# Linear attention ahead of two feed-forward layers: regrouping four kinds of small fp32 matmuls

## Chip, cores and metric

One core of a Trainium2 chip runs the whole program. The metric is the device time of one execution in microseconds (us).

## What is computed

The reference chains three layers; the change is in the first.

```python
def _attn_ref(q, k, v, w_phi):            # q, k, v: 4 batches x 8 heads x 576 x 64; w_phi 64 x 128
    def phi(x):
        proj = np.einsum('bhsd,df->bhsf', x, w_phi)
        proj = proj - np.max(np.abs(proj), axis=-1, keepdims=True)
        return np.concatenate([np.exp(proj), np.exp(-proj)], axis=-1)
    q_p, k_p = (phi(q), phi(k))
    kv = np.einsum('bhsf,bhsd->bhfd', k_p, v)
    z = np.sum(k_p, axis=2)
    num = np.einsum('bhsf,bhfd->bhsd', q_p, kv)
    den = np.einsum('bhsf,bhf->bhs', q_p, z)[..., None] + 1e-06
    return num / den
```

Its output, 2304 tokens of 512 features, goes through a feed-forward layer (512 to 2048 and back, the hidden values squared after the relu) and then through eight gated feed-forward experts (512 to 1024 and back) whose gates are balanced in eight rounds.

## The kernel before

Attention works in 16 units of two heads each (four units make a batch). A unit has ten steps: `kT` and `kp` (turn k, project it, take exponentials: tiles `ek`, made in three pieces, the last of 64 rows), `qst`, `qT` and `qp` (split, turn and project q, take the maximum over features with GpSimd's all-reduce, take exponentials: four tiles `eq`), `kv` (function `kv_sum`), `kz` (`kv_turn`), `num` (`numerators`), `rec` and `fin`. A list written by hand, `OFFS`, with a period `TU` of 17.54, sets in which order the steps are traced. A scheduler then fixes the order on each engine at build time: it takes what is ready, in the order of tracing. On the chip every engine runs its list in order.

`kv_sum` adds up `v^T ek` for two heads in the upper and lower 64 partitions of a PSUM tile `kvp`, over five row tiles (four of 128 rows and one of 64), and the column sums of `ek` in `zp`, whose stationary operand is 32 columns of ones: four of these matmuls fill the 128 partitions. Each fp32 matmul of this kind is two instructions in the trace. Before, the row tiles go in pairs, `kvp` first and then `zp` for the pair. ScalarE copies both to `kvs`; `kv_turn` transposes them into `kzp`, from which VectorE makes `kv` and `z`.

`numerators` makes for each half `c` of the tokens the numerators `psn` (64 columns of `kv`, two heads side by side) and the denominators `psd` (32 columns of `z`, four matmuls side by side). ScalarE copies them to `nm` and `dn`. Two DMAs gather the denominators in `comp`, VectorE inverts them, one DMA writes them to DRAM (`rden`), two read them back spread over partitions (`rb`), and `finish` multiplies, rounds to `xh` (ScalarE) and keeps the rest in `xl` (VectorE).

PSUM tiles `kvp`, `zp`, `kzp`, `psn` and `psd` share three banks (`pc`, `PCB = 3`). The four `eq` tiles of a unit have four buffers (`EQB = 4`), so those of the next unit take the place of the ones that `psn` and `psd` have read.

The matmuls of the first feed-forward pass (`first_l1`, `first_l2`, PSUM tile `ps`, by blocks of 288 tokens) come after attention in the order of tracing and fill gaps in it. `HOLD` keeps some blocks back until `kv` of a named unit is through; its anchor is the last `zp` matmul that `kv_sum` returns. The weights' decoding (lines 198 to 204) sits on VectorE beside attention.

Of the kernel before, what the change touches and what calls it, by code (L numbers as in the profile page):

```python
# [8 lines left out]
F32 = mybir.dt.float32  # L9
# [11 lines left out]
def tile_features_attention__moe__sinkhorn_moe(  # L21
# [18 lines left out]
    nc = tc.nc  # L40
    P = 128
    B, H, S, D = q.shape
    NT, DM = out.shape
    NF = w_phi.shape[1]
# [10 lines left out]
    MT = S // P  # L55
# [39 lines left out]
    pc = a1.enter_context(tc.tile_pool(name="pc", bufs=PCB, space=PSUM, reuse_waits="tile"))  # L95
# [13 lines left out]
    ones = const.tile([P, P], F32, name="ones")  # L109
# [27 lines left out]
    def load_v(u):  # L137
        load_kv(u, v, "v", VAB)
# [195 lines left out]
    def kv_sum(u, eks):  # L334


        t = nat.pop(("v", u))
        kvp = pc.tile([P, 512], F32, tag="pc", name="kvp")
        zp = pc.tile([P, 512], F32, tag="pc", name="zp")

        def rows(i, h):
            r = P if i < MT else R0
            return r, eks[i // GT][:r, i % GT, h].rearrange("p a f -> p (a f)")

        for g in range(0, MT + 1, 2):
            tiles = range(g, min(g + 2, MT + 1))
            for i in tiles:
                for h in range(2):
                    r, e = rows(i, h)
                    nc.tensor.matmul(  # L350
                        kvp[h * D : (h + 1) * D, : 2 * NF], t[:r, i, h], e, start=(i == 0), stop=(i == MT)
                    )
            for i in tiles:
                for h in range(2):
                    r, e = rows(i, h)
                    q0 = 32 * (2 * (i % 2) + h)
                    ins = nc.tensor.matmul(  # L357
                        zp[q0 : q0 + 32, : 2 * NF], ones[:r, :32], e, start=(i < 2), stop=(i >= MT - 1)
                    )
        load_v(u + VAB)  # L360
        kvs = ab.tile([P, 2, 2, NF], F32, tag="kvs", name="kvs")
        nc.scalar.copy(kvs[:, 0].rearrange("p a f -> p (a f)"), kvp[:, : 2 * NF])
        nc.scalar.copy(kvs[:, 1].rearrange("p a f -> p (a f)"), zp[:, : 2 * NF])
        return kvs, ins.ins

    def kv_turn(u, kvs):
# [30 lines left out]
    def numerators(u, kz, eqs):  # L397

        kv, z = kz
        nm = ab.tile([P, 2, HALF], F32, tag="nm", bufs=NMB, name="nm")  # L400
        dn = ab.tile([P, 2, HALF], F32, tag="dn", name="dn")
        for c in range(2):
            ps = pc.tile([P, 512], F32, tag="pc", name="psn")
            for a in range(2):
                for h in range(2):
                    nc.tensor.matmul(  # L406
                        ps[h * D : (h + 1) * D, :HALF], kv[:, a, h * D : (h + 1) * D], eqs[2 * c + h][:, a],
                        start=(a == 0), stop=(a == 1),
                    )
            nc.scalar.copy(nm[:, c], ps[:, :HALF])  # L410
            ps = pc.tile([P, 512], F32, tag="pc", name="psd")
            for a in range(2):
                for h in range(2):
                    q0 = 32 * (2 * h + a)
                    nc.tensor.matmul(  # L415
                        ps[q0 : q0 + 32, :HALF], z[:, a, h], eqs[2 * c + h][:, a], start=True, stop=True
                    )
            nc.scalar.copy(dn[:, c], ps[:, :HALF])
        comp = ab.tile([P, 2, NT2], F32, tag="comp", bufs=1, name="comp")
        for a in range(2):  # L420
            nc.sync.dma_start(comp[:, a], dn[32 * a : P : 64].rearrange("p c s -> p (c s)"))
        return nm, comp
# [18 lines left out]
    def first_l1(pool, t0, n, fs=range(NFT)):  # L441
        return [split_square(pool, layer1(0, f, t0, n), n, HALF) for f in fs]
# [33 lines left out]
    def s_kv(u):  # L476
        U[u]["kvs"], U[u]["kvi"] = kv_sum(u, U[u].pop("ek"))
# [4 lines left out]
    def s_num(u):  # L482
        U[u]["nm"], U[u]["comp"] = numerators(u, U[u].pop("kz"), U[u].pop("eq"))
# [18 lines left out]
    for u in range(NU):  # L502
        t = u * TU
# [9 lines left out]
    for i, (t0, n) in enumerate(halves[:-2]):  # L513
        with ExitStack() as es:
            if i in HOLD:
                es.enter_context(tc.issue_after(U[HOLD[i][0]][HOLD[i][1]]))
            g = ahead + first_l1(hp, t0, n, range(len(ahead), NFT))
# [12 lines left out]
    with tc.tile_pool(name="hp1t", bufs=1, reuse_waits="tile") as hpt:  # L530
        g = [ahead + first_l1(hp, *halves[-2], range(len(ahead), NFT)), first_l1(hpt, *halves[-1])]
# [195 lines left out]
    for p in range(1, N1):  # L727
# [10 lines left out]
        for bi, (t0, n) in enumerate(blocks):  # L738
            g = []
# [294 lines left out]
    for n in range(NN):  # L1034
        l2 = layer2(n)
        if n + 1 < NN:
            l1 = layer1(n + 1)
            p, q = order[n + 1]
# [75 lines left out]
```

## Time and profile before

| | |
|---|---|
| median of 3 runs | 2109.71 us (2109.64 to 2115.81) |
| the profiled execution | 2112.68 us, of which the span is 2110.9 us |
| mean granted TensorE clock over the span | 0.991 |
| PE busy, share of the span | 98% |
| attention: first projection to last `xl` | 6.9 us to 306.5 us |

The page gives for each engine its busy time. PE are the matmuls, PEld the weight loads, DVE is VectorE, ACT ScalarE and POOL GpSimd. In a timeline each line has the start, the time to the end of the last instruction of the group, the engine, the line of the kernel, the operation, out<-in, the weights' shape (rows*columns), the moving operand, and how many instructions there are. A time in square brackets is how long the engine stood idle before it, and what ended the wait. Matmuls overlap, so the distance from start to start says what one costs.

### The profile page before, as it was taken

The numbers are of one execution on the slowest core, as the hardware profiler recorded it, in microseconds if no ns is written. First come the engines' busy times: TensorE is split into PE (matmuls) and PEld (weight loads), VectorE is DVE, ScalarE is ACT, GpSimd is POOL, SyncE is SP. The second block draws the span as 40 slices with busy tenths as digits, with TensorE's granted clock in tenths as the row PEclk, the third lists the DMA queues.
The fourth block names the chain that finished last, engine by engine and source line by source line (L and its number), as shares of the span: only waits on it lengthen the run. The fifth ranks groups of instructions, "written<-read, shape, count | busy, mean of one in ns | idle before, by whom it ended". The sixth has DMA issues, their size and how long they took to land.

```text
span 2110.9 us, 31778 instructions
## 1 busy us (share of the span) xinstructions
PE 2070.3 (98%) x12411; PEld 1933.7 (92%) x12411; DVE 1737.5 (82%) x2162; ACT 873.6 (41%) x1503; POOL 773.3 (37%) x425
## 2 busy tenths in 40 slices
PE   8999999999999899999999999999999999999998
PEld 5556679888999899999999999999999999999998
DVE  5888665776556787999989889899898998989986
ACT  6786744222233554433434334343343333433332
POOL 3343300010104444444544435444444444444431
PEclk9999999999999999999999999999999999999999
DMA  4444241100134557667766677666766667666663
GB/s 116 103 108 120 72 126 60 60 31 31 55 143 173 200 178 243 195 243 247 229 220 212 227 250 224 228 217 219 252 225 220 225 223 242 224 227 225 221 200 122
DMA packets 184052, 376.40 MB, mean 178 GB/s; under 512 B 73440, under 2 KB 114272, under 8 KB 183904
## 3 DMA queue, kind: packets, MB, share of 16 engines
q1 hardware_dynamic: 183904, 374.38, 53.9%
q8 instruction: 99, 1.62, 0.3%
q14 instruction: 49, 0.40, 0.1%
HBM read 349.26 MB, written 24.93 MB: 177 GB/s over the span
## 4 chain that ended last, share of the span: by engine, by line
PE 87%; DVE 7%; DMA 3%; ACT 1%; issue 1%; SPq 1%; POOL 0%; DVEq 0%; ACTq 0%
PE psa L855 31%; PE psb L855 31%; PE ps L241 6%; PE ps L242 6%; PE ps L243 6%; PE kvp L350 1%; DMA rb<-rden 1%; PE psn L406 1%; PE zp L357 1%; DVE xl L591 1%; PE psg L632 1%; DMA rden<-comp 1%; PE psd L415 1%; DVE xh L591 1%; DVE acc L971 1%
## 5 line engine op out<-in xcount | busy, mean ns | idle before, releaser
L855 PE MATMUL psa<-xl,xh 128*128 128x384 f32 x2400 | 446.8, 335 | 6.4 <-DVE xl L591 2.5
L855 PE MATMUL psb<-xl,xh 128*128 128x384 f32 x2400 | 444.2, 334 | 2.9 <-DVE xl L591 2.1
L855 PEld LDWEIGHTS psa<-xl,xh 128*128 128x128 f32 x2400 | 419.5, 188 | 8.1 <-DVE xl L591 2.9
L855 PEld LDWEIGHTS psb<-xl,xh 128*128 128x128 f32 x2400 | 418.3, 188 | 3.5 <-DVE xl L591 2.4
L883 POOL TENSOR_TENSOR t<-r,r 128x768 f32<-128x768 f32 x96 | 208.3, 2170 | 500.0 <-DVE r L923 453.1
L883 POOL TENSOR_TENSOR t<-r,t 128x768 f32<-128x768 f32 x96 | 236.6, 2464 | 5.6 <-DVE r L923 1.9
L591 DVE TENSOR_TENSOR xl<-t,xl 128x768 fp32r<-128x768 f32 x128 | 185.1, 1446 | 1.7 <-ACT xl L590 1.7
L971 DVE TENSOR_TENSOR acc<-psb,acc 128x768 f32<-128x768 f32 x163 | 155.0, 951 | 38.2 <-PE psb L855 34.7
L971 DVE TENSOR_TENSOR acc<-psa,acc 128x768 f32<-128x768 f32 x161 | 153.0, 950 | 38.6 <-PE psa L855 35.5
L855 PE MATMUL psb<-xl,w2v 128*128 128x384 f32 x960 | 180.3, 335 | 0.0
L855 PE MATMUL psa<-xl,w2v 128*128 128x384 f32 x960 | 179.7, 334 | 0.0
L590 ACT CAST xl<-t 128x768 fp32r<-128x768 f32 x128 | 107.4, 839 | 152.8 <-POOL t L883 62.3
L855 PEld LDWEIGHTS psb<-xl,w2v 128*128 128x128 f32 x960 | 168.0, 188 | 0.0
L855 PEld LDWEIGHTS psa<-xl,w2v 128*128 128x128 f32 x960 | 167.5, 188 | 0.0
L590 ACT CAST xl<-r 128x768 fp32r<-128x768 f32 x96 | 80.6, 839 | 156.1 <-PE psa L855 79.2
L390 POOL PARTITION_ALL_REDUCE eq<-eq x64 | 91.0, 1465 | 136.9 <-ACT eq L389 136.9
L591 DVE TENSOR_TENSOR xl<-r,xl 128x768 fp32r<-128x768 f32 x96 | 136.6, 1423 | 2.8 <-ACT xl L590 2.8
L241 PE MATMUL ps<-xh,w0h 128*128 128x288 f32 (+3 forms) x384 | 133.5, 348 | 3.2 <-ACT r L262 2.9
L242 PE MATMUL ps<-xl,w0h 128*128 128x288 f32 (+3 forms) x384 | 131.5, 343 | 0.0
L243 PE MATMUL ps<-xh,w0l 128*128 128x288 f32 (+3 forms) x384 | 131.5, 344 | 0.0
L661 POOL TENSOR_TENSOR s<-wf 128x512 f32<-128x512 f32 x32 | 44.5, 1391 | 227.3 <-PE ps L243 82.4
L242 PE MATMUL ps<-gl,w1h 128*128 128x288 f32 (+3 forms) x384 | 126.3, 336 | 0.0
(193 smaller groups left out, 3832.2 us busy)
## 6 DMA issues: line engine op xcount, KB each, us to landing
xl<-xv SPq DMA_DIRECT2D x329, 768.0 KB
wf<-in_moe_w_dram SPq DMA_DIRECT2D x32, 1024.0 KB
gate<-prT SPq DMA_DIRECT2D x45, 384.0 KB
xv<-xvs SPq DMA_DIRECT2D x14, 768.0 KB
raw<-in_moe_w_in_dram SPq DMA_DIRECT2D x16, 512.0 KB
raw<-in_moe_w_out_dram SPq DMA_DIRECT2D x16, 512.0 KB
xv<-xl SPq DMA_DIRECT2D x7, 768.0 KB
qnat<-in_q_dram SPq DMA_DIRECT2D x16, 288.0 KB
```

The lines of the kernel that those rows point to most:

```text
L241: nc.tensor.matmul(ps, ah, bh, start=first, stop=False)
L242: nc.tensor.matmul(ps, ah, bl, start=False, stop=False)
L243: nc.tensor.matmul(ps, al, bh, start=False, stop=last)
L350: nc.tensor.matmul(kvp[h * D : (h + 1) * D, : 2 * NF], t[:r, i, h], e, start=(i == 0), stop=(i == MT))
L357: ins = nc.tensor.matmul(zp[q0 : q0 + 32, : 2 * NF], ones[:r, :32], e, start=(i < 2), stop=(i >= MT - 1))
L390: nc.gpsimd.partition_all_reduce(eq[:, 1], eq[:, 0], P, bass_isa.ReduceOp.absmax)
L590: nc.scalar.copy(v[:, 0], src)
L591: nc.vector.tensor_sub(v[:, 1], src, v[:, 0].bitcast(F32))
L661: nc.gpsimd.tensor_tensor(s1, a(2, 1), a(2, 2), ALU.add)
L855: ins = nc.tensor.matmul(ps[:, x, :NB], w[:, wi, k, cs], b[:, bi, k], start=first and k + i == 0, stop=k == KH - 1 and i == 2, skip_group_ ...
L883: nc.gpsimd.tensor_tensor(t[nm], x, y, ALU.subtract)
L971: latest["dve"] = nc.vector.tensor_add(o, ps, o).ins
```

## The change

`kv_sum` now puts both sums in the two halves of one bank, `kvz`; it does all matmuls of `kvp` and then all of `zp`, from the last row tile (64 rows) to the first, and `zp` is tied behind the last `kvp`. One ScalarE copy of 128x512 takes the place of two of 128x256. `numerators` does both halves' `psn`, then both halves' `psd`, with the second half and the second head first.

```diff
-        kvp = pc.tile([P, 512], F32, tag="pc", name="kvp")
-        zp = pc.tile([P, 512], F32, tag="pc", name="zp")
+        kvz = pc.tile([P, 2, 2 * NF], F32, tag="pc", name="kvz")
+        kvp, zp = kvz[:, 0], kvz[:, 1]
...
-        for g in range(0, MT + 1, 2):
-            tiles = range(g, min(g + 2, MT + 1))
-            for i in tiles:
-                for h in range(2):
-                    r, e = rows(i, h)
-                    nc.tensor.matmul(
-                        kvp[h * D : (h + 1) * D, : 2 * NF], t[:r, i, h], e, start=(i == 0), stop=(i == MT)
-                    )
-            for i in tiles:
+        for i in range(MT, -1, -1):
+            for h in range(2):
+                r, e = rows(i, h)
+                ins = nc.tensor.matmul(
+                    kvp[h * D : (h + 1) * D], t[:r, i, h], e, start=(i == MT), stop=(i == 0)
+                )
+        with tc.issue_after(ins.ins):
+            for i in range(MT, -1, -1):
                 for h in range(2):
                     r, e = rows(i, h)
                     q0 = 32 * (2 * (i % 2) + h)
                     ins = nc.tensor.matmul(
-                        zp[q0 : q0 + 32, : 2 * NF], ones[:r, :32], e, start=(i < 2), stop=(i >= MT - 1)
+                        zp[q0 : q0 + 32], ones[:r, :32], e, start=(i >= MT - 1), stop=(i < 2)
                     )
         load_v(u + VAB)
         kvs = ab.tile([P, 2, 2, NF], F32, tag="kvs", name="kvs")
-        nc.scalar.copy(kvs[:, 0].rearrange("p a f -> p (a f)"), kvp[:, : 2 * NF])
-        nc.scalar.copy(kvs[:, 1].rearrange("p a f -> p (a f)"), zp[:, : 2 * NF])
+        nc.scalar.copy(kvs.rearrange("p b a f -> p b (a f)"), kvz)
...
-        for c in range(2):
+        for c in (1, 0):
             ps = pc.tile([P, 512], F32, tag="pc", name="psn")
             for a in range(2):
-                for h in range(2):
+                for h in (1, 0):
...
             nc.scalar.copy(nm[:, c], ps[:, :HALF])
+        for c in (1, 0):
             ps = pc.tile([P, 512], F32, tag="pc", name="psd")
             for a in range(2):
-                for h in range(2):
+                for h in (1, 0):
```

## Rows read from the trace of the kernel before

**Rows 1.** The page: busy time, share and instructions of each engine.
```profile
PE 2070.3 (98%) x12411; PEld 1933.7 (92%) x12411; DVE 1737.5 (82%) x2162; ACT 873.6 (41%) x1503; POOL 773.3 (37%) x425
```
**Rows 2.** Stretches: length, busy us of each engine, granted clock, DMA share, GB/s.
```profile
0.00:305.00 305.00, 289.70 (x2240) 188.74 (x2240) 227.02 (x479) 211.34 (x544) 102.93 (x85) 0.98 0.40 101
76.00:84.00 8.00, 8.00 (x47) 4.11 (x43) 5.17 (x13) 4.36 (x13) 2.08 (x3) 0.50 0.34 72
240.00:260.00 20.00, 20.00 (x158) 14.12 (x157) 15.97 (x35) 13.87 (x35) 5.29 (x5) 1.00 0.20 58
```
**Rows 3.** One stretch by tile (kvp, zp, psn, psd): busy PE, PEld, ACT.
```profile
0.00:300.00 300.00, 46.69 (x320) 20.43 (x320) 5.90 (x16) 0.98 0.39 99
0.00:300.00 300.00, 30.99 (x320) 8.92 (x320) 6.01 (x16) 0.98 0.39 99
0.00:300.00 300.00, 41.53 (x256) 16.50 (x256) 11.96 (x32) 0.98 0.39 99
0.00:300.00 300.00, 24.16 (x256) 5.43 (x256) 12.71 (x32) 0.98 0.39 99
```
**Rows 4.** Timeline of PE, second part of the numerators of the fourteenth unit.
```profile
249.19 0.69 PE L415 MATMUL psd<-eq,z 128*32 128x288 f32 x8
249.81 1.19 PE L406 MATMUL psn<-eq,kv 128*64 128x288 f32 x8
250.93 0.40 PE L386 MATMUL psq<-qT,wks 128*128 128x288 f32 x1
...
251.70 0.29 PE L241 MATMUL ps<-xh,w0h 128*128 128x288 f32 x1
251.83 0.30 PE L242 MATMUL ps<-xl,w0h 128*128 128x288 f32 x1
252.05 0.69 PE L415 MATMUL psd<-eq,z 128*32 128x288 f32 x8
252.68 0.40 PE L243 MATMUL ps<-xh,w0l 128*128 128x288 f32 x1
252.91 0.29 PE L241 MATMUL ps<-xh,w0h 128*128 128x288 f32 x1
```
**Rows 5.** Timeline of PE, `kv_sum` of the fifteenth unit.
```profile
254.75 0.62 PE L357 MATMUL zp<-ek,ones 128*32 128x256 f32 x2
...
255.76 0.63 PE L357 MATMUL zp<-ek,ones 128*32 128x256 f32 x6
...
258.24 1.08 PE L350 MATMUL kvp<-ek,vnat 128*64 128x256 f32 x8
259.25 0.64 PE L357 MATMUL zp<-ek,ones 128*32 128x256 f32 x8
259.82 0.65 PE L350 MATMUL kvp<-ek,vnat 64*64 64x256 f32 x4
260.40 0.62 PE L357 MATMUL zp<-ek,ones 64*32 64x256 f32 x4
```
**Rows 6.** Timeline of PE, `kvp` of the third unit, unbroken.
```profile
44.63 2.53 PE L350 MATMUL kvp<-ek,vnat 128*64 128x256 f32 x20
```
**Rows 7.** ScalarE copies out of PSUM, by shape: count, busy us, mean ns.
```profile
L296 ACT CAST qT<-psqT 128x512 fp32r<-128x512 f32 x32 | 18.7, 589 | 3.1 <-PE psqT L295 2.5
...
L362 ACT COPY kvs<-kvp 128x256 f32<-128x256 f32 x16 | 5.9, 369 | 7.3 <-PE kvp L350 7.2
```
**Rows 8.** Timeline of VectorE and PE around 72 us.
```profile
72.50 0.76 DVE L436 TENSOR_TENSOR nm<-nm,rb 128x576 f32<-128x576 f32 x1 [3.04 <-DMA rb<-rden]
...
74.32 3.86 PE L350 MATMUL kvp<-ek,vnat 128*64 128x256 f32 x20 [2.01 <-ACT dn L418]
```
**Rows 9.** Timeline of GpSimd, the all-reduces of the ninth and tenth units.
```profile
138.67 6.60 POOL L390 PARTITION_ALL_REDUCE eq<-eq  x4 [4.55 <-ACT eq L389]
...
152.31 1.24 POOL L390 PARTITION_ALL_REDUCE eq<-eq  x1 [4.54 <-ACT eq L389]
```
**Rows 10.** Timeline of PE behind the last unit of attention.
```profile
307.43 0.61 PE L241 MATMUL ps<-xh,w0h 128*128 128x288 f32 x1 [2.88 <-ACT r L262]
```

## Prediction

> **What bounds the kernel now.** I read the page first: PE is busy for 98% of the span and every other engine has room [rows 1]. All that the change touches lies in the first 305 us, so I took that stretch next: PE 289.7 of 305 us, VectorE 227, ScalarE 211, GpSimd 103 [rows 2]. Of the 15 us in which PE stands, most is the start (attention's first projection comes at 6.9 us); in the stretch from 240 to 260 us it stands for nothing at all. What PE does in the rest of the first 305 us is attention, with the first feed-forward blocks in its gaps; these have to be done anyway, so a microsecond of PE that attention gives back can be used as long as a block is ready to fill it. The bound of this stage is thus mostly PE. It is not PE alone: the attention chain through ScalarE, GpSimd, VectorE and two round trips by DMA stops PE at some places, which the last two parts come back to.
>
> Busy is not the same as useful for the four small matmul kinds. I took their timelines, since start to start shows the price of a group. `kvp` x8 takes 1.01 us (258.24 to 259.25) and x4 takes 0.58 [rows 5], so four instructions (two matmuls side by side) stream in 0.43 us and each group pays 0.15 on top. `zp` x8, four side by side, takes 0.57: 0.43 and 0.14. The unbroken `kvp` x20 is busy for 2.53 us [rows 6]; less the 0.07 by which a group's last instruction overlaps the next one (1.08 against 1.01), that is 5 x 0.43 and two surcharges, one for the four row tiles of 128 and one for the tile of 64 rows. `psn` x8 takes 1.12 and `psd` x8 0.62 [rows 4]: 0.485 for each round and about 0.14 for each group. Beside that, an excursion out of ordinary 128-column matmuls costs at its ends: these follow each other at 0.13 us, the last one before `psd` at 0.22 and the first one after it at 0.23 [rows 4], so 0.19 for each excursion.
>
> **The change part by part.** *Grouping in `kv_sum`.* The fifteenth unit has its sums in seven groups: a `kvp` x8 (20 instructions a unit, 12 of them shown), `zp` x2, `zp` x6, `kvp` x8, `zp` x8, `kvp` x4, `zp` x4, in four excursions [rows 5]. The changed order allows four groups in one excursion: `kvp` x4 and x16, `zp` x4 and x16, busy for 2.53 and for 2 x 0.15 + 3 x 0.43 + 0.07 = 1.66 us.
>
> *Grouping in `numerators`.* Four groups, here in about three excursions since matmuls of other steps stand ahead of each half's `psd` or behind it [rows 4], become two in one: 0.15 + 4 x 0.485 + 0.07 = 2.16 and 0.15 + 2 x 0.485 + 0.07 = 1.19 us.
>
> *The sum at best.* The four tiles keep PE busy for 46.7 + 31.0 + 41.5 + 24.2 = 143.4 us now [rows 3]. New: 16 x (2.53 + 1.66 + 2.16 + 1.19) = 120.6. Of the difference of 22.8, some 3 us are `kvp` and `zp` of the fifth unit at half clock (3.86 us for 2.53 [rows 6, 8]), which need not go, and 5 groups fewer in each of 16 units take 80 x 0.07 = 5.6 of overlap with them that was never lost: 14.2 stay. Excursions: units like those shown go from seven to two; others are less broken (the third unit's `kvp` is whole [rows 6]), so I take 3.5 fewer on average: 16 x 3.5 x 0.19 = 10.6. Together 25 us at best.
>
> *What I keep of it.* The scheduler may still put a ready matmul of an earlier traced step (a projection of q, a transpose) into each block. One more group and excursion in each of two blocks a unit costs 16 x 2 x (0.15 + 0.19) = 11. I take 14 us of PE, between 8 (more breaks) and 25.
>
> By the Trainium skill, page TensorEngine Tiling (Array Packing), section Key Properties, changing the tiling mode drains TensorE, while another tile of the same mode does not. By that rule the order of heads within a group is worth nothing and the 64-row tile costs a surcharge in either order; the sum above has it the same way, and no row here shows the array draining.
>
> *One bank and one copy.* Two ScalarE copies of 0.37 us become one of 128x512, for which the nearest row is 0.59 [rows 7]: 16 x 0.15 = 2.4 us of ScalarE, which has room. But the copy of the first sum can't run beside the second sum any more; the end of `zp` to the end of the copies becomes 0.59 in place of 0.37 where the first copy was early, 0.22 a unit, at most 3.5 us over 16 units if nothing covered it. I take nothing: feed-forward and projection matmuls stand behind `zp` on PE. Without that cover it is the 3.5.
>
> The Trainium skill, page PSUM — Partial Sum Buffer, section PSUM bank collisions raise a hardware error, says that two engines must not be in the same bank and quadrant at once, even at different columns. By that rule the early copy is lost for good, and the sum would be 3.5 us worse at most; no run here shows the collision.
>
> *Fewer banks.* A unit takes six `pc` tiles in place of seven, and `kv_sum` one in place of two. At 74.32 us PE has waited 2.01 with `kvp` for a bank that ScalarE's copy `dn` had yet to empty [rows 8]. The copy is late since ScalarE's list has `xh` ahead of it, which waits for VectorE, which waited 3.04 us for the DMA `rb`. One bank fewer makes that wait rarer but doesn't mend its cause; nothing counted, up to 2 us of gain at such a place.
>
> *Last-made operand first.* PE's first matmul of each block now waits for the last `ek` or `eq`, and whatever stands behind it in PE's list waits too. The scheduler places a block when its first matmul is ready, so the others go through without waiting. The price is on the ring of `eq` buffers: before, the first two came free after the first `psn` and `psd`, 1.12 + 0.62 us into the block; now after both `psn` and one `psd`, 2.1 + 0.6. The next unit's all-reduces wait for them (4.55 and 4.54 us idle, ended by the ScalarE copy into `eq` [rows 9]). At least about 1 us a unit is added where this ring sets the pace, since the other two buffers come free about when they did and GpSimd needs 6 us for four anyway (6.60 for x4 [rows 9]); at most some 2.5, if every all-reduce moves with the first. The nothing at the other end: where the period is longer than the ring. All-reduces of the ninth and tenth units start 13.6 us apart [rows 9], while 300 us over 16 units are 18.8; so I count it in about a quarter of the units, 4 x 1 = 4 us.
>
> *Moved DMAs.* The two DMAs into `comp` still follow the second `dn` on SP's queue, and the load of the next v still follows the last `zp`. No queue is passed.
>
> The sum: 14 less, 4 back, 10 us less than the profiled 2112.68 us (span 2110.9 and 1.8 around it): 2102.7. That execution is 3.0 above the median of the runs, 2109.7, so for a median I forecast 2100.
>
> **The rivals.** *It does nothing for the end.* Attention's pace is set by its chain, not by PE, and PE's savings become waits. For it: behind the last unit PE stood 2.88 us [rows 10], where VectorE's list, too, hangs on `rb`; blocks held back by `HOLD` can't fill earlier gaps. Against it: no idle PE from 240 to 260. Time: 2109.7, give or take 5.
>
> *More than forecast.* The blocks stay whole (25 us), and a stall like that at 72 us goes. With it goes a slow stretch: the granted clock was 0.50 from 76 to 84 us, the 1.2 GHz level, after the wait of 2.01 us [rows 2, 8]; 8 us at half speed are 4 lost. The Trainium skill, page TensorE: Matmul & The Clock Gate, section HAM oscillation — how this bites in real kernels, says that idle gaps between bursts lower the clock; by that rule the trace agrees at this place. 25 + 2 + 4, less the 4 of the ring, are 27: 2083.
>
> *Slower: the ring of `eq`.* If the full 2.5 us is passed on, and the ring sets the pace in seven of the first ten units, attention's early part grows by 17 us, while PE's 14 us can be used only in the nine others (14 x 9 / 16 = 8). Time: 2109.7 + 17 - 8 = 2119. It decides from about 1.1 us a unit over seven units on. For it: POOL's waits [rows 9], and a first-half block that used to run before the second half's exponentials. Against it: most periods are longer than 13.6 us.
>
> **How the numbers follow.** Forecast 0.42, nothing for the end 0.25, more 0.13, slower 0.20. What a measurement can tell from no change is about 0.3%, 6.3 us. Faster by more: nearly all of the first (0.38), all of the third and a little of the second (0.03), 0.54. Slower: three quarters of the last (0.15) and 0.04 of the second, 0.19. Within: 0.27. The forecast's own range is 2090 to 2106; the range to hold 8 in 10 reaches to the rivals' times, 2083 and 2119.
>
> **What would show it.** Right: `kvp` and `zp` groups of x16 and x20 and `psn` x16 in the timeline, busy time of the four tiles near 125 to 130 us in place of 143, last `xl` of attention some 10 us earlier, no more idle PE than now. Wrong: that busy time down but idle PE up by as much, starting at `kvp` or `psn` waits for ScalarE's exponentials; all-reduces further apart than 13.6 us in the early units; or groups still broken up.

## The result, and the profile after

The changed kernel takes 2129.63 us (median of 6 runs, 2128.55 to 2131.08), the kernel before 2111.32 beside it (6 runs): a ratio of 1.0082, 95% interval 1.0065 to 1.0099. It is slower by 17 us, where 2100 us, some 10 us less than before, was forecast; it lies outside the range, which ended at 2119.

The page's line of the engines, to be held against [rows 1]:

```profile
PE 2064.6 (97%) x12411; PEld 1934.5 (91%) x12411; DVE 1743.7 (82%) x2162; ACT 872.5 (41%) x1487; POOL 769.3 (36%) x425
```

PE is busy for 5.7 us less, and yet the span is 2127.7 in place of 2110.9 us: PE stands 22.5 us more. The windows of the first 305 us, and below them of the tiles `kvz`, `psn` and `psd` alone over all of attention, which answer to [rows 2, 3]:

```profile
core 0: us, PE busy (x) PEld busy (x) DVE busy (x) ACT busy (x) POOL busy (x), PEclk, DMA share, GB/s
0.00:305.00 305.00, 267.59 (x2118) 175.62 (x2120) 218.15 (x452) 203.82 (x512) 99.67 (x85) 0.98 0.38 95
...
core 0: us, PE busy (x) PEld busy (x) ACT busy (x), PEclk, DMA share, GB/s
0.00:325.00 325.00, 68.39 (x640) 29.86 (x640) 9.25 (x16) 0.98 0.39 100
...
0.00:325.00 325.00, 37.36 (x256) 18.14 (x256) 11.98 (x32) 0.98 0.39 100
...
0.00:325.00 325.00, 22.16 (x256) 5.06 (x256) 12.81 (x32) 0.98 0.39 100
```

The tiles' busy time is 127.9 us, against 143.4 before. Three of the four kinds of block did become whole: in the order of PE's instructions `kvp` stands unbroken in 14 of the 16 units (4 before), `zp` in 14 (6 before) and `psn` in all (none before); `psd` came in two parts in every unit. But PE is busy for 267.6 of the first 305 us, against 289.7: 22.1 us of the extra standing lie there. Attention's last `xl` ends at 324.2 us, against 306.5, and behind it the two kernels run alike (1803.5 and 1804.4 us to the end). Where PE stands, by what ended the wait (sum, times, longest), from 30 to 300 us, the four longest of the changed kernel and, below them, the longest of before:

```profile
engine line waited for: us in total, times, longest us
PE psq L386 <- DVE ek L328: 9.5, 10, 2.7
PE psn L406 <- ACT eq L393: 4.5, 5, 1.0
PE kzp L370 <- ACT kvs L363: 3.1, 4, 1.3
PE psd L416 <- ACT dn L419: 1.8, 2, 1.3
...
PE kvp L350 <- ACT dn L418: 5.2, 4, 2.4
```

This view of the changed kernel adds up to 26.3 us, the same view of before to 7.6, of which 5.2 are `kvp` behind `dn`. That wait is gone; others on all sides have come. No single one explains 17 us. Two stretches of PE's timeline say more: the first unit (two lines of before stand ahead of it), and the sums over k of the eighth, with the last of ScalarE's exponentials that they read.

```profile
start us, us, engine line op out<-in xcount [idle before <-releaser]
11.96 1.08 PE L350 MATMUL kvp<-ek,vnat 128*64 128x256 f32 x8 [0.72 <-ACT ek L330]
...
20.09 0.70 PE L406 MATMUL psn<-eq,kv 128*64 128x288 f32 x2 [0.35 <-ACT eq L393]
...
14.81 0.44 PE L387 MATMUL psq<-qT,wks 128*128 128x288 f32 x1
15.18 3.70 PE L350 MATMUL kvz<-ek,vnat 64*64 64x256 f32 x20
...
25.92 2.16 PE L406 MATMUL psn<-eq,kv 128*64 128x288 f32 x16
28.01 0.69 PE L416 MATMUL psd<-eq,z 128*32 128x288 f32 x8
...
29.10 0.69 PE L416 MATMUL psd<-eq,z 128*32 128x288 f32 x8
...
137.40 0.44 ACT L330 ACTIVATE ek<-ek 64x256 f32<-64x256 f32 x1
...
138.10 2.53 PE L350 MATMUL kvz<-ek,vnat 64*64 64x256 f32 x20
140.56 1.62 PE L358 MATMUL kvz<-ek,ones 64*32 64x256 f32 x20
142.11 0.63 PE L295 MATMUL psqT<-ident_r,qst 128*128 128x128 f32 x5
142.58 0.35 PE L241 MATMUL psk<-wdh,kh 128*128 128x256 f32 x1
```

`kvz` x20 in 2.53 and 1.62 and `psn` x16 in 2.16 are as predicted; `psd` is not, with x8 twice for the x16 forecast. What is late is the blocks' place. Before, the first unit's sums began at 11.96 us, on the first piece of `ek`, and its numerators at 20.09; now they begin at 15.18 and 25.92. The eighth unit's sums begin 0.26 us after ScalarE's last exponential for them, which ran from 137.40 to 137.84, and the next unit's `psk` stands behind them. GpSimd's first all-reduces of the units around it, for [rows 9]:

```profile
134.73 1.42 POOL L390 PARTITION_ALL_REDUCE eq<-eq  x1 [8.06 <-ACT eq L389]
...
150.72 5.88 POOL L390 PARTITION_ALL_REDUCE eq<-eq  x4 [7.25 <-ACT eq L389]
...
167.98 5.09 POOL L390 PARTITION_ALL_REDUCE eq<-eq  x4 [8.08 <-ACT eq L389]
```

They are 16.0 and 17.3 us apart, against 13.6 for the two of before in [rows 9]. These distances scatter from unit to unit (11.6 to 22.5 us before, 14.6 to 24.1 now); the mean of all fifteen is 17.3 us before and 18.3 now.

### The profile page after: what moved, and what is told of

It reads as the page before. It is cut to its first block, busy times and chain, and to the rows that moved or that the text cites. A ratio compares the mean times of both kernels' runs of the same rounds, so it can differ in the third digit from the quotient of the medians.

```text
span 2127.7 us, 31767 instructions
## 1 busy us (share of the span) xinstructions
PE 2064.6 (97%) x12411; PEld 1934.5 (91%) x12411; DVE 1743.7 (82%) x2162; ACT 872.5 (41%) x1487; POOL 769.3 (36%) x425
## 3 DMA queue, kind: packets, MB, share of 16 engines
q8 instruction: 99, 1.62, 0.3%
## 4 chain that ended last, share of the span: by engine, by line
PE 81%; DVE 9%; DMA 5%; ACT 2%; issue 1%; SPq 1%; POOL 0%; DVEq 0%; ACTq 0%
PE psa L856 30%; PE psb L856 30%; PE ps L241 6%; PE ps L242 6%; PE ps L243 6%; DMA rb<-rden 2%; DVE xl L592 1%; DMA xl<-xv 1%; DVE acc L972 1%; DMA rden<-comp 1%; PE psn L406 1%; PE kvz L350 1%; PE psg L633 1%; DMA comp<-dn 1%; DVE w2v L592 1%
## 5 line engine op out<-in xcount | busy, mean ns | idle before, releaser
L972 DVE TENSOR_TENSOR acc<-psa,acc 128x768 f32<-128x768 f32 x161 | 153.0, 950 | 39.9 <-PE psa L856 36.7
L243 PE MATMUL ps<-gh,w1l 128*128 128x288 f32 (+3 forms) x384 | 126.2, 336 | 0.4 <-DVE w1l L237 0.2
```

The source lines that it names most:

```text
L243: nc.tensor.matmul(ps, al, bh, start=False, stop=last)
L972: latest["dve"] = nc.vector.tensor_add(o, ps, o).ins
```

## The experiments

The theories, in the order in which they came up. A: the ring of `eq` buffers holds the next unit back. B: the sums over k begin too late, since the last-made operand goes first. C: the ring of the one `nm` buffer. D: the grouping takes away short pieces of work that PE did while other matmuls waited. E: any change of the lists would cost as much. F: the rings of `ek` and `eq` hold one unit each, and the reversed order frees the first-made buffer last. G: no ring, the late start of each block is what costs.

**The two parts alone.** `e1_kv_only` has the changed `kv_sum` and the `numerators` of before; `e2_num_only` the other way round.

> The sums grouped, in one bank and from the last tile on, with the numerators of before. Theory A (the ring of four eq buffers): the loss is all in the numerators, so this one is faster than before by what its groups give back on PE, some 5 to 10 us (ratio 0.995 to 0.998). Theory B (the sums start too late, since they wait for the last exponentials of k): slower by about as much as the whole change, 10 to 18 us.

> The numerators grouped and from the last half on, with the sums of before. Theory A: slower by at least as much as the whole change, 17 to 25 us, with the first all-reduces of successive units 16 to 18 us apart in the early units as after the change. Theory B: same as before or faster, 0 to 8 us less.

Measured: e1 2125.27 us, ratio 1.0072 (1.0049 to 1.0095); e2 2140.65, 1.0152 (1.0135 to 1.0169). Each part alone costs, and the two don't add up; e2 lost more than either theory had. A, which put the loss into the numerators, can't be all of it.

**The order inside the numerators.** Two forms on top of the changed `kv_sum`: `e3_num_fwd` keeps the grouping and runs first-made first; `e4_num_half_rev` gives up the grouping and keeps the reversed order.

```diff
 e3_num_fwd
-        for c in (1, 0):
+        for c in (0, 1):
-                for h in (1, 0):
+                for h in (0, 1):
```

> The whole change, but halves and heads in the order in which they are made; still both numerators, then both denominators. Theory A: psn of the first half can start 4 to 5 us earlier, but its buffers come free only after psd, which stands behind the other half's psn and so behind the last exponential: nearly as slow as the change, 12 to 17 us over before. If the order alone were at fault: within 3 us of before.

> The whole change, but numerators and denominators half by half again, last half and head first. Theory A: the block waits for the last exponential as in the change and the first two buffers come free only one psn (1 us) sooner: 10 to 16 us over before. If the grouping alone were at fault: within 3 us of before or faster.

Measured: e3 2126.11, 1.0082 (1.0062 to 1.0101); e4 2130.43, 1.0096 (1.0079 to 1.0112). With the changed sums over k in place, the form of the numerators hardly matters.

**The rings of nm and eq, and the start.**

```diff
 e5_nm_ring2
-    NMB = 1
+    NMB = 2
-HB = {"hh": 5, "hl": 5, "r": 1}
+HB = {"hh": 4, "hl": 4, "r": 1}
 e6_eq_ring5
-    EQB = 4
+    EQB = 5
-HB = {"hh": 5, "hl": 5, "r": 1}
+HB = {"hh": 4, "hl": 4, "r": 1}
```

`e7_den_first` puts the loop over `psd` and its copies ahead of the loop over `psn`; `e8_kv0_before` calls the `kv_sum` of before for unit 0.

> The changed kernel with two buffers for nm instead of one; the room comes from hh and hl, which get 4 buffers instead of 5. Theory C (with one nm buffer, the copy of a unit's numerators waits for the end of the unit before; in the changed kernel this waiting copy stands ahead of the copies of the denominators on ScalarE, so the DMA round trip of the denominators is shut into the same ring): the period of the units falls from 17.5 to at most 16.3 us and the kernel comes to 2105 to 2116 us. Theory A (the ring of eq buffers holds back the all-reduces of the next unit): within 3 us of the changed kernel, 2127 to 2133. Theory B (the sums over k begin too late, at the start above all): no gain either.

> The changed kernel with five buffers for eq instead of four, with room from the same place (hh and hl with 4 buffers). Theory A: the first all-reduce of a unit no longer waits 4.4 to 5.4 us behind the last exponential of the unit before, and the kernel comes to 2109 to 2118 us. Theory C: within 3 us of the changed kernel, 2127 to 2133, as the nm copy still sets the period.

> The changed kernel, but both denominators and their copies first, then both numerators and theirs; nothing else differs. Theory C: the copies of the denominators no longer stand behind the nm copies, the DMA round trip of a unit runs while the unit before is finished, and the kernel comes to 2105 to 2118 us. Theory A: the eq buffers come free by the last numerators instead of the last denominators, no sooner: 2125 to 2133 us. Theory B: 2125 to 2133 us.

> The changed kernel, but the first unit's sums with k and v are those of before (two banks, tile pair by tile pair, first tile first); units 1 to 15 are as changed. Theory B, for the start: the first numerators come at 20 us instead of 26 and the kernel gains about 6 us, 2121 to 2125. Theories A and C: the gain at the start is taken up by the rings behind it in part; 2123 to 2130 us.

Measured: e5 2130.64, 1.0080 (1.0065 to 1.0095); e6 2130.22, 1.0078 (1.0061 to 1.0094); e7 2135.70, 1.0114 (1.0097 to 1.0131); e8 2134.50, 1.0095 (1.0080 to 1.0111). No gain in any; e7 and e8 came out 3 and 5 us slower than any theory had them. C falls by e5 and e7; against A stands e6, with one `eq` buffer more. In e8 the first unit's sums began at 12.04 us again, but its numerators, which still ask for the last `eq` first, only at 29.64, later even than in the changed kernel (25.92), for which no run gives the reason: what the first block gained did not reach the second.

**Grouping against order.** `e9_kv_fwd` is the kernel before with the sums grouped in one bank and one copy, first tile first; `e10_num_fwd_only` the kernel before with the numerators grouped, first-made first; `e11_before_h4` the kernel before with `hh` and `hl` at 4 buffers and nothing else; `e12_pa4_pc2` the changed kernel with `PAB, PCB = 4, 2`.

```diff
 e9_kv_fwd
-        for g in range(0, MT + 1, 2):
-            tiles = range(g, min(g + 2, MT + 1))
...
+        for i in range(MT + 1):
...
+        with tc.issue_after(ins.ins):
+            for i in range(MT + 1):
```

> The kernel before, with the sums over k grouped in one bank as in the change, but from the first row tile to the last; numerators as before. Theory B (the sums start too late, since the last-made operand goes first): the loss of 15 us goes with the order, 2108 to 2114 us. Theory D (what costs is the grouping: PE's list, worked off in order, has lost the short pieces of sums that stood between matmuls which have to wait for ScalarE and VectorE, and PE stands there): the loss stays, 2119 to 2128 us.

> The kernel before, with both halves' numerators ahead of both denominators, first-made operand first; sums over k as before. Theory D: the second half's numerators bring the list to a stand before the first denominators; a loss like that of the last-made order, 2125 to 2140 us. Theory B (the order of the operands costs, not the grouping): 2105 to 2115 us.

> The kernel before with no other edit than 4 buffers in place of 5 for hh and hl, the feed-forward's rounded blocks. No instruction is added, taken away or moved in the text; only the scheduler's lists shift. Theory E (the lists of the kernel before happen to fit the chip, and any other lists leave PE standing more): 2118 to 2135 us, with 15 us more of idle PE before 340 us. Theories B and D: 2107 to 2115 us, as the loss belongs to the edits themselves.

> The changed kernel with four banks for the projections and transposes (pa) and two for the sums (pc), in place of three and three: the change uses one bank fewer for the sums, and this gives it to the tiles where PE waits most (psq behind VectorE's subtraction that empties psk, 9.5 us in ten waits). Theory D in its narrow form (this wait is what the lost filling matmuls had covered): 9 us less than the changed kernel, 2117 to 2122. Theory E: the wait moves to other tiles, 2123 to 2140 us.

Measured: e9 2111.73, 0.9996 (0.9981 to 1.0012); e10 2117.13, 1.0028 (1.0015 to 1.0042); e11 2111.37, 1.0001 (0.9987 to 1.0015); e12 2140.47, 1.0142 (1.0117 to 1.0166). This is the turn. The same grouped sums cost nothing in the forward order (e9) and 0.72% in the reversed one (e1); the numerators 0.28% (e10, 2 us above the range of B and far below that of D) against 1.52% (e2). D falls for the sums, and E with e11: lists shifted by another edit alone changed nothing. In e12 a bank more for `psk` and `psq` and one less for the sums was worse, and PE's wait at `psq`, from 30 to 300 us, grew from 9.5 to 25.8 us (first line below); since one ring got what the other lost, e12 alone does not say what the bank is worth. That this wait came with the order is seen in e13, further down: there it is 0.4 us, with the banks of the changed kernel (second line).

```profile
PE psq L386 <- DVE ek L328: 25.8, 22, 2.1
...
PE psq L386 <- DVE ek L328: 0.4, 1, 0.4
```

**Everything as changed, but forward; and wider rings.** `e13_fwd_both` joins e9 and e10. `e14_ek_ring` is the changed kernel with this line, and `hh` and `hl` at 4:

```diff
-            ek = ab.tile([P, GT, 2, 2, NF], F32, tag="ek", bufs=EKB, name="ek")
+            ek = ab.tile([P, n, 2, 2, NF], F32, tag="ek" if n == GT else "ekr", bufs=EKB if n == GT else 1, name="ek")
```

`e15_kv_fwd_ek_ring` has the same on top of e9; `e16_both_rings` has it with `EQB = 5` and `VAB = 1` on the changed kernel, so one buffer fewer for v.

> The changed kernel with its grouping, its one bank and its one copy, but every loop over row tiles, halves and heads runs first-made first. Theory B (the order is the cause): the sum of its two parts measured alone, 0.9996 and 1.0028, so 2109 to 2119 us; about 15 us faster than the changed kernel. Theory D (the grouping of both together costs): 2124 us or more.

> The changed kernel with a wider ring for ek: the third piece of a unit, of 64 rows, gets a buffer of its own, so three buffers are left for the two large pieces; the room comes from hh and hl with 4 buffers. Theory F (the ring of ek holds exactly one unit; last-made first gives the first-made piece back last, so the next unit's ek begins only when the sums are through): the next unit's first subtraction into ek moves ahead of the end of the sums, the period falls from 18.0 to 16.5 us or less, 2108 to 2120 us. Theory G (it is no ring, but each block simply ends later after its last operand, and the next unit's projection of k stands behind it in PE's list): 2126 to 2134 us.

> The kernel before with the sums over k grouped in one bank, first tile first, and the wider ring for ek of the experiment above. Theory F: if the ring of ek sets the period of 16.2 us in the kernel before too, it falls, and the kernel gains 2 to 8 us on 2111, bounded by the idle of PE there: 2103 to 2109. Theory G: 2108 to 2114 us.

> The changed kernel with both rings wider: ek as above and five buffers for eq; the room comes from hh and hl with 4 buffers and from one buffer for v in place of two, which can delay the load of v. Theory F with both rings (widening one alone leaves the other to set the pace): 2105 to 2118 us. Theory G: 2124 to 2135 us.

Measured: e13 2108.33, 0.9981 (0.9966 to 0.9995); e14 2133.06, 1.0108 (1.0087 to 1.0129); e15 2114.41, 1.0021 (1.0008 to 1.0033); e16 2128.50, 1.0091 (1.0068 to 1.0114). With the order alone undone, the whole loss is gone, 21 us, and 4 us are gained on the kernel before, less than the 6.3 us that the prediction took as the least a measurement can tell. Rings wider by one buffer give nothing: F falls as far as these runs go, whichever ring or both. PE's timeline of e13, first unit and ninth:

```profile
start us, us, engine line op out<-in xcount [idle before <-releaser]
...
12.13 1.08 PE L350 MATMUL kvz<-ek,vnat 128*64 128x256 f32 x8 [0.72 <-ACT ek L330]
...
14.03 1.66 PE L350 MATMUL kvz<-ek,vnat 128*64 128x256 f32 x12
15.62 1.07 PE L358 MATMUL kvz<-ek,ones 128*32 128x256 f32 x16
...
20.57 0.67 PE L406 MATMUL psn<-eq,kv 128*64 128x288 f32 x2 [0.61 <-DVE zs L375]
...
139.69 1.95 PE L350 MATMUL kvz<-ek,vnat 128*64 128x256 f32 x16
141.57 0.27 PE L308 MATMUL pskT<-ident,knat 64*128 64x64 f32 x1
141.78 0.65 PE L350 MATMUL kvz<-ek,vnat 64*64 64x256 f32 x4
142.35 1.62 PE L358 MATMUL kvz<-ek,ones 128*32 128x256 f32 x20
...
149.01 1.68 PE L406 MATMUL psn<-eq,kv 128*64 128x288 f32 x8
...
151.87 0.70 PE L406 MATMUL psn<-eq,kv 128*64 128x288 f32 x2
...
153.58 1.19 PE L406 MATMUL psn<-eq,kv 128*64 128x288 f32 x6
```

The first sums start at 12.13 and the first numerators at 20.57, both on what is there; the ninth unit's four large tiles are summed from 139.69 on, while ScalarE is still at the last exponentials (one runs from 139.82, the last from 140.63 to 141.06). The numerators are broken up again (x8, x2, x6): in e13 `psn` stands unbroken in 5 of the 16 units and `kvp` in 3, `zp` in 15.

**Late start or reversed order?** Both kernels are e9 with another list of row tiles; tile 4 is the one of 64 rows, made last.

```diff
 e17_kv_gate
-        for i in range(MT + 1):
+        for i in (4, 0, 1, 2, 3):
 e18_kv_rev_no_gate
-        for i in range(MT + 1):
+        for i in (3, 2, 1, 0, 4):
```

> The kernel before with the grouped sums over k in one bank; the last row tile (64 rows, made last) goes first, the other four follow first-made first. Theory G (the late start of the block costs): as with the full reversed order, 2122 to 2130 us. Theory F (the reversed order of reading and freeing costs): 2108 to 2115 us.

> The kernel before with the grouped sums over k in one bank; the four row tiles of 128 go last-made first, and the last tile (64 rows, made last of all) comes last. The block needs the second of three pieces to begin, not the third. Theory G: most of the loss goes, 2109 to 2117 us. Theory F: it stays, 2121 to 2130 us.

Measured: e17 2132.91, 1.0105 (1.0087 to 1.0123); e18 2115.61, 1.0019 (1.0008 to 1.0031). Four of the 20 instructions of a sum, moved from the end to the front, cost 21 us against e9 (the time is 3 us above the range of G); reversing the other 16 costs 4, and there the intervals overlap. G stands. Not all of the 21 us is PE standing, though: in the profiled executions PE stands 13.4 us more in e17 than in e9 (56.5 and 43.1), and is busy 14.8 us more (2074.2 and 2059.4) for the same 12411 instructions, with a mean granted clock of 0.989 against 0.997. ScalarE's first exponentials of e17 for the sums, and PE's timeline at the start:

```profile
start us, us, engine line op out<-in xcount [idle before <-releaser]
11.29 0.63 ACT L330 ACTIVATE ek<-ek 128x512 f32<-128x512 f32 x1
...
13.74 0.94 ACT L330 ACTIVATE ek<-ek 128x512 f32<-128x512 f32 x2
...
15.00 4.68 PE L351 MATMUL kvz<-ek,vnat 64*64 64x256 f32 x20
19.62 1.17 PE L359 MATMUL kvz<-ek,ones 64*32 64x256 f32 x6
```

The sums start 3.0 us later than in e9 (12.00), though the two tiles of the first piece are ready at 11.92 us; the last exponentials end at 14.68.

The table puts the kernels together. "Sums" is the start of a unit's first sum less the end of its last exponential of k; "numerators" the start of its first `psn` or `psd` less the end of its last exponential of q (both the mean over ten units from the third on; negative: the block starts before its last operand is there). "Period" is a tenth of the time from the end of the second unit's sums to the end of the twelfth's. These are taken from the starts and ends of those instructions in the trace. "PE stands" is the span less PE's busy time, and "clock" the mean granted TensorE clock, both of the one profiled execution; the ratio is of the medians of several runs.

| kernel | sums, us | numerators, us | period, us | last `xl` ends, us | PE stands, us | clock | ratio |
|---|---|---|---|---|---|---|---|
| before | -0.21 | -0.43 | 16.2 | 306.5 | 40.6 | 0.991 | 1 |
| e9, sums forward | -1.34 | -0.73 | 16.2 | 302.4 | 43.1 | 0.997 | 0.9996 |
| e13, both forward | -1.47 | -0.59 | 16.1 | 302.0 | 39.9 | 0.991 | 0.9981 |
| e18, reversed, last tile last | -0.35 | -0.67 | 16.3 | 308.0 | 44.0 | 0.991 | 1.0019 |
| e10, numerators forward | -0.67 | -0.34 | 16.7 | 314.0 | 44.7 | 0.991 | 1.0028 |
| e1, sums reversed | 0.88 | 1.21 | 17.4 | 319.8 | 54.4 | 0.994 | 1.0072 |
| changed | 1.47 | 1.58 | 18.0 | 324.2 | 63.1 | 0.992 | 1.0082 |
| e17, last tile first | 0.56 | 1.02 | 18.3 | 326.5 | 56.5 | 0.989 | 1.0105 |
| e2, numerators reversed | 1.42 | 0.72 | 18.8 | 334.6 | 55.3 | 0.984 | 1.0152 |

Where the blocks start before their last operand in the mean, the period is 16.1 to 16.7 us and PE stands 40 to 45 us; where they start after it, 17.4 to 18.8 and 54 to 63. The eleven kernels that are not in the table fall on the same two sides (e11 and e15 with periods of 15.6 and 16.2 us, the others 17.7 to 19.4). Single units scatter: before, too, four of the ten sums begin after their last operand. A late block of one kind makes the other late too: in e1 the numerators are those of before, in e2 the sums.

## Why the prediction was wrong

*The blocks on PE: right but for `psd`.* `psn` x16 in 2.16, `kvz` x20 in 2.53 and 1.62 (forecast 2.16, 2.53, 1.66), tiles busy for 127.9 us (125 to 130); `psd` x16 in 1.19 never came. The saving was 15.5 us by these rows, and 10 after the 5.6 of overlap that the prediction takes off; it kept 14, with 8 as the low end. Excursions out of other matmuls fell from 88 to 53 in PE's list, 2.2 a unit where 3.5 were taken. PE's whole busy time fell by only 5.7; the other 4 came back in other matmuls, which I did not follow.

*One bank and one copy: right at nothing.* In e9 both sums share a bank and have one copy, and the ratio is 0.9996 with what the grouping saves on PE in it. By the Trainium skill, page PSUM — Partial Sum Buffer, section PSUM bank collisions raise a hardware error, the copy of the first sum can no longer run beside the second; e9 shows no price for that, but a small one could hide behind the grouping's gain.

*Fewer banks: the stall is gone* (`kvp` behind `dn`, 5.2 us in the stretch from 30 to 300 us), as was thought possible, and it did not pay.

*Last-made operand first: this step failed.* The prediction says that the scheduler places a block when its first matmul is ready, "so the others go through without waiting. The price is on the ring of `eq` buffers", and books 4 x 1 = 4 us. The first half is what happened, and the mistake was to take it as free. A block that asks for its last operand first gives up the time in which it ran beside the making of its operands, in each of the 16 units and in both blocks, and the prediction has no term for that, for the sums over k none at all. It costs 21 us (e13 against the changed kernel, 2108.33 and 2129.63), five times the 4 booked, and a wider ring of the kind named gives none of it back (e6, e16). Between e13 and the changed kernel the clock hardly differs (0.991 and 0.992); PE stands 23.2 us more. The sum that read 14 less and 4 back comes out at 4 less and 21 back. The rows shown ahead of the prediction had a hint: `kvp` and `zp` came in seven groups in a unit [rows 5], which the prediction read as waste. They were also the sums following the exponentials as these came: the first of them began 1.5 us before the last exponential ended.

*The grouping's worth: too large.* With forward order it brings 4 us (e13: 0.9981, 1 to 7 by the interval) where 14 were kept. Without the reversed order neither `psn` nor `kvp` stays whole: the tiles' busy time is 137.5 us in e13, so that of the 15.5 us saved in the changed kernel 5.9 are left; and e10 shows the numerators grouped at a loss of 0.28%. What made the blocks whole and what made them late was the same edit, which the prediction did not see.

*The rivals.* "Slower" named the right sign, 2119 us, with the wrong mechanism as far as the runs go: with one `eq` buffer more the loss stays (e6). "Wrong" was foreseen as busy time down and idle PE up, starting at waits of `psn` for ScalarE's exponentials; that is seen (4.5 us), as part of a wider delay.

*Left open:* how the late block becomes a longer period. In 15 of 15 steps from unit to unit, before and after and in e13, the next unit's first `psk` starts after the last sum of the unit before, so a late sum hands its delay on along PE's list; but no run here moved `psk` ahead of the sums, so this link is argued, not shown. Against the rings of `nm`, `eq` and `ek` as the link stand e5, e6, e14 and e16, each with one buffer more.

## What to carry to other kernels

When an accumulation reads operands that another engine is still making, its order decides when it may start: ask of each reordered block which operand is made last, and give the overlap that is lost a price of its own; PE's busy time does not show it (5.7 us less here, in a kernel slower by 17). Grouping and order are separate edits; e13 takes what of the first is left without the second and is the fastest of all kernels here, if by 0.2%. When PE's busy time falls and its standing grows by more, look for one tile whose place changed: in e17 four instructions of twenty were enough for 13.4 us of standing and a loss as large as that of the whole change.

## What the runs showed that I had not expected

That the two parts don't add: the changed sums alone cost 0.72%, the changed numerators alone 1.52%, both together 0.82%. Part of this is the clock and not the wait: over the first 305 us the mean granted clock was 0.94 in e2, against 0.98 before, in e1 and after the change, and of the 27.6 us by which e2's profiled execution is longer than that of before, 14.7 are PE standing and 12.9 are more busy time for the same instructions. By standing alone the parts cost 13.8 (e1), 14.7 (e2) and, together, 22.5 us, which still don't add up. And that the late start in the first unit met a slow stretch: its `kvz` x20 took 3.70 us for the usual 2.53, with a mean granted clock of 0.72 from 14 to 20 us, so partly at the 1.2 GHz level, after PE had stood for 1.01 and 0.56 us; in e13 the mean clock was 1.00 from 14 to 20 us. In e17 the same block took 4.68 us, although the view has a granted clock of 1.00 from 15 to 20 us; this stays open.
